# Routing by prefix-scan instructions, and table entries that serve as row numbers, in an attention, mixture-of-experts and convolution kernel

## The chip, the cores and the metric

The kernel runs on one core of one Trainium2 chip. The core has five engines that run side by side, each in its own program order: TensorE (PE, matrix products; PEld is its weight load), VectorE (DVE), ScalarE (ACT), GpSimd (POOL) and SyncE (SP, which here only issues transfers). The metric is the device time of one execution in microseconds (us); lower is better. Times are the median over separate executions; the trace and the page come from one further execution under the profiler.

## The reference, cut to what matters

Four sequences of 576 tokens pass through a windowed attention (8 heads of 64), a mixture of 8 experts with sticky routing, and a gated convolution layer. The part that the change touches is the routing:

```python
logits = x @ w_gate
for s in range(S):
    fresh_e = argmax(logits[b, s])
    if s == 0 or local_gate[b, s] < 0.5:
        e = fresh_e
    else:
        e = prev_e
    prev_e = e
    out[b, s] = p[e] * (relu(x[b, s] @ w1[e]) @ w2[e])
```

So a token keeps the expert of the last token before it that chose afresh, and each expert works on the rows of the tokens that it got.

## The kernel before, in words

Attention runs first, in a loop of 40 groups and 5 more steps, `t` = 0 to 44. Step `t` issues, in this order: the scores `s` of group t (`stage_a`, with the masked maximum `sm` on DVE, four instructions per group, two where a group is a half), the transposes `tpq`/`tpk` for the next head pair, the subtraction `sm<-sm,mx` on POOL (`stage_sub`), every fifth step the router products `lp` (`stage_l`), the transposes `pt` of group t-2 (`stage_b`), transposes `tpx` of finished rows (`stage_d`), the output products `o` of group t-3 (`stage_c`, with `rc`, a reciprocal and `xsb` on DVE where three slots are full), and the exponential of group t on ACT.

The routing of sequences 0 and 1 (`route(0)`, started at t = 25) and of 2 and 3 (`route(1)`, t = 44) is a chain of about a hundred small DVE instructions with four matrix products in it. Tokens lie as 72 partitions by 8 (`PJ`) by 2 sequences. The chain's DVE instructions wait in a list (`Later.todo`); `tick` sends one of them after certain DVE instructions of attention, and `tick(REST)` three at the end of a step. The four products are `lg` (the logits), `wp` (the running maximum carried across partitions), `bt` (counts carried across partitions) and `tb` (the table of row numbers). A product is issued when the list is empty and the loop passes the place that `PLACES` names for it: place 0 stands ahead of `pt`, place 1 ahead of `o`, place 2 behind `o`. What reads a product is issued by `early`, after two (`EVACUATE`) later calls of `passed`, of which each step has three. In the order lists this decides where each of them stands; nothing is reordered on the chip.

The running maximum over the 8 tokens of a partition is made by three shifted steps between two `scans` buffers, the running counts of the 8 experts by a copy and three shifted steps between two `ranks` buffers:

```python
for sh in (1, 2, 4):
    a, n = bufs[cur], bufs[1 - cur]
    later.tensor_tensor(out=n[:, :, 4:], in0=a[:, :, 4:], in1=a[:, :, 4 - sh : 4 + PJ - sh], op=ALU.max)
```

The table `tab` holds row number plus one, zero in an empty place. `lanes_of` and `pick1` make two index lists of it: `idx` (entry minus one, not below zero) for the gather of rows from `xD`, and `sidx` (entry minus one, and row 2304 for an empty place) for the scatter of results to `yD`, which has one row more than there are tokens.

PSUM buffers are shared by tag: `pt`, `tpx` and `bt` of `route(0)` take turns in two buffers, `s`, `lp`, `lg` and `tb` in two others, `o` and `wp` in two others.

From t = 37 on POOL gathers rows for the first expert segment (`xg`), PE turns them (`xt`), and the expert layers follow (`up`: products `h`, evacuated by ACT `hh` and DVE `hl`; `down`: products `yf` and `y`). Weights come as f32 (`wst`) and are split into two f16 halves by ACT (`wh`) and DVE (`wl`). `route(1)` runs beside the first expert segment, with PE at `h` and `yf`.

Of the kernel before, what the change touches and what calls it, by code (L numbers as in the profile page):

```python
# [10 lines left out]
F16 = mybir.dt.float16  # L11
# [11 lines left out]
N = B * S  # L23
# [41 lines left out]
PLACES = (1, 0, 0, 2)  # L65
# [22 lines left out]
def _consts():  # L88
# [38 lines left out]
    add("ie", one * np.tile(np.arange(E), 2 * PJ)[None])  # L127
    add("ik", one * np.repeat(np.arange(E), E)[None])
# [14 lines left out]
    add("tokx", np.concatenate([np.stack([(PJ * p + j) + 0.0 * b, np.full((PP, PJ), b), np.ones((PP, PJ))], -1).reshape(PP, -1) for b in range(B)], 1))  # L143
# [17 lines left out]
def attention_moe_conv_kernel(ctx: ExitStack, tc: tile.TileContext, q, k, v, w_gate, w_local, w1, w2, w_val, conv_w, w_out, consts, out):  # L161
# [4 lines left out]
    xD = dram.tile([N, D], F32, name="xD")  # L166
# [43 lines left out]
    oh_all = cp.tile([PP, B, PJ, E], F32, name="oh_all")  # L210
# [27 lines left out]
    idx8, sidx8 = r2([P, E, TILES], "idx8", I32), r2([P, E, TILES], "sidx8", I32)  # L238
# [63 lines left out]
    def cols_of(g, which):  # L302
        k, t0, n = SEGS[g]
        if k in (0, 2):
            ix = idx[k, t0 > 0][which]
            return lambda t: ix[:, t : t + 1]
        ix = (idx8, sidx8)[which]
        return lambda t: ix[:, k, t0 + t : t0 + t + 1]

    def gather(g, n=None, col=None, tiles=None):  # L310
        if col is None:
            n, col = SEGS[g][2], cols_of(g, 0)
        r = []
        for t0, m in tiles_of(n)[tiles or slice(None)]:
            x = xg.tile([P, D], F32, tag="xg", name=f"xg{g}_{t0}")
            G.indirect_dma_start(out=x[:m], out_offset=None, in_=xD[0 : 2 * S if g in (0, 1) else N, :], in_offset=bass.IndirectOffsetOnAxis(ap=col(t0 // P)[:m], axis=0))
            r.append(x)
        return r
# [41 lines left out]
    def down(g, k=None, n=None, pool=None, col=None):  # L360

        if n is None:
            k, _, n = SEGS[g]
            col = cols_of(g, 1)
# [44 lines left out]
    def turn_y(g):  # L409
        n, col = SEGS[g][2], cols_of(g, 1)  # L410
# [18 lines left out]
    if True:  # L429
# [11 lines left out]
        scans = [rt.tile([PP, 2, 4 + PJ], F32, name=f"scan{n}") for n in range(2)]  # L441
        ranks = [rt.tile([PP, 2, 4 + PJ, E], F32, name=f"ranks{n}") for n in range(2)]
# [10 lines left out]
        for u in scans:  # L453
            G.memset(u[:, :, 0:4], 0.0)
        for u in ranks:
            G.memset(u[:, :, 0:4, :], 0.0)
# [223 lines left out]
        class Later:  # L680
# [7 lines left out]
            def __getattr__(self, name):  # L688
                return getattr(Deferred(self.todo, V), name)

# [53 lines left out]
        def route(bp):  # L744
# [43 lines left out]
            later.tensor_tensor(out=dg, in0=ident[:PP, :PP].unsqueeze(1).to_broadcast([PP, 2, PP]), in1=vm[:, :, 3 + PJ : 4 + PJ].to_broadcast([PP, 2, PP]), op=ALU.mult)  # L788
# [10 lines left out]
            later.tensor_tensor(out=es, in0=vm[:, :, 4:], in1=bc(car, PJ), op=ALU.max)  # L799
            later.tensor_scalar(out=es, in0=es, scalar1=E - 1, scalar2=None, op0=ALU.bitwise_and)  # L800
            oh = oh_all[:, 2 * bp : 2 * bp + 2]
            esf = es.rearrange("p b j -> p (b j)")
            ohf = oh.rearrange("p b j e -> p (b j) e")
            ief = c("ie", PP).rearrange("p (j e) -> p j e", j=BJ)
            later.tensor_tensor(out=ohf, in0=ief, in1=bc(esf, E), op=ALU.is_equal)
# [23 lines left out]
            r3 = t([PP, 2, PJ, E], "r3")  # L829
            later.tensor_tensor(out=r3, in0=inc[:, :, 4:, :], in1=bt.unsqueeze(2).to_broadcast([PP, 2, PJ, E]), op=ALU.add)  # L830
# [5 lines left out]
            r3f = r3.rearrange("p b j e -> p (b j) e")  # L836
            later.tensor_tensor(out=r3f, in0=r3f, in1=ohf, op=ALU.mult)
            rk = rank_all[:, 2 * bp : 2 * bp + 2].rearrange("p b j -> p (b j)")
            later.tensor_reduce(out=rk, in_=r3f, axis=AX.X, op=ALU.add)
# [32 lines left out]
            for h in range(2 * bp):  # L872
# [4 lines left out]
                later.tensor_tensor(out=exps[h], in0=exps[h], in1=oh_all[:, 2 * h : 2 * h + 2].rearrange("p b j e -> p (b j) e"), op=ALU.mult)  # L877
# [6 lines left out]
        def lanes_of(nm, js, t0, t1):  # L884
# [5 lines left out]
            ixf, emp = r2([P, k, n], f"ixf{nm}"), r2([P, k, n], f"emp{nm}")  # L890
            later.tensor_reduce(out=ixf, in_=pr, axis=AX.X, op=ALU.add)
            i, o = r2([P, k, n], f"idx{nm}", I32), r2([P, k, n], f"sidx{nm}", I32)
# [737 lines left out]
```

## Time and profile before

| | |
|---|---|
| time, median of 3 executions | 459.72 us (459.29 to 461.29) |
| time of the profiled execution | 461.68 us |
| its span (first to last instruction) | 459.9 us |
| mean granted TensorE clock | 0.989 of full speed |
| busy: PE, PEld, DVE, ACT, POOL | 438.2, 326.5, 341.4, 292.6, 163.2 us |
| instructions: PE, DVE, POOL | 4618, 1006, 192 |

PE is busy for 95% of the span, so time can be won only where PE waits or where its clock is lowered. Busy time of the other engines matters where they make PE wait.

### The profile page before, as it was taken

The numbers are of one execution on the slowest core, as the hardware profiler recorded it, in microseconds if no ns is written. First come the engines' busy times: TensorE is split into PE (matmuls) and PEld (weight loads), VectorE is DVE, ScalarE is ACT, GpSimd is POOL, SyncE is SP. The second block draws the span as 40 slices with busy tenths as digits, with TensorE's granted clock in tenths as the row PEclk, the third lists the DMA queues.
The fourth block names the chain that finished last, engine by engine and source line by source line (L and its number), as shares of the span: only waits on it lengthen the run. The fifth ranks groups of instructions, "written<-read, shape, count | busy, mean of one in ns | idle before, by whom it ended". The sixth has DMA issues, their size and how long they took to land. (4 is left out here: it accounts for less than half of the span.)

```text
span 459.9 us, 12133 instructions
## 1 busy us (share of the span) xinstructions
PE 438.2 (95%) x4618; PEld 326.5 (71%) x4618; DVE 341.4 (74%) x1006; ACT 292.6 (64%) x590; POOL 163.2 (35%) x192
## 2 busy tenths in 40 slices
PE   8899999889699999999999999999999999999997
PEld 7567777556476578875788888788785857666664
DVE  5667787889758883787979898997138788779730
ACT  2887888676845233546666757767347998785532
POOL 3666665323600251402313232242005755434130
PEclk9999999899979999999999999999999999999999
DMA  9978598457637484378858897981043323020202
GB/s 212 208 173 198 130 250 201 131 143 229 216 91 261 161 273 157 96 209 274 263 181 295 277 328 232 329 275 59 9 153 103 126 71 125 24 93 1 93 21 95
DMA packets 56868, 77.79 MB, mean 169 GB/s; under 512 B 25809, under 2 KB 34017, under 8 KB 56806
## 3 DMA queue, kind: packets, MB, share of 16 engines
q1 hardware_dynamic: 53430, 67.18, 49.5%
q0 software_dynamic: 3232, 9.72, 6.1%
q8 instruction: 38, 0.62, 0.6%
q14 instruction: 24, 0.20, 0.1%
q10 hardware_dynamic: 144, 0.07, 0.1%
HBM read 62.65 MB, written 14.30 MB: 167 GB/s over the span
## 5 line engine op out<-in xcount | busy, mean ns | idle before, releaser
L347 PE MATMUL h<-xh,wh 128*128 128x256 f16 (+9 forms) x352 | 87.0, 257 | 2.5 <-DVE hl L351 2.2
L347 PE MATMUL h<-xl,wh 128*128 128x256 f16 (+9 forms) x352 | 86.9, 257 | 0.1
L347 PE MATMUL h<-xh,wl 128*128 128x256 f16 (+9 forms) x352 | 86.9, 257 | 0.0
L269 DVE SCALAR_TENSOR_TENSOR wl<-wst,wh 128x1024 f16<-128x1024 f32 x64 | 77.9, 1220 | 10.1 <-ACT wh L264 9.9
L1477 DVE SCALAR_TENSOR_TENSOR acc<-y,cw,acc 128x288 f32<-128x288 f32 x128 | 65.6, 520 | 9.2 <-ACT acc L1451 6.3
L347 PEld LDWEIGHTS <-wh 128*128 128x128 f16 x704 | 64.5, 98 | 10.9 <-issue 3.9
L264 ACT ACTIVATE wh<-wst 128x1024 f16<-128x1024 f32 x64 | 67.0, 1050 | 2.4 <-DMA wst<-in_moe_w_dram 2.4
L349 ACT ACTIVATE hh<-h 128x256 f16<-128x256 f32 (+9 forms) x88 | 30.7, 349 | 44.6 <-PE h L347 42.0
L579 POOL TENSOR_TENSOR sm<-sm,mx 128x384 f32<-128x384 f32 (+1 forms) x40 | 32.6, 815 | 52.4 <-DVE mx L571 35.2
L351 DVE SCALAR_TENSOR_TENSOR hl<-h,hh 128x256 f16<-128x256 f32 (+9 forms) x88 | 32.3, 376 | 25.4 <-ACT hh L349 24.8
L358 POOL DMA_INDIRECT yD<-yr,sidx x15 | 17.4, 1159 | 85.5 <-ACT yr L357 56.6
L396 PE MATMUL yf<-wh,hh 128*128 128x512 f16 x104 | 39.4, 379 | 0.1
L396 PE MATMUL yf<-wl,hh 128*128 128x512 f16 x104 | 39.4, 379 | 0.0
L396 PE MATMUL yf<-wh,hl 128*128 128x512 f16 x104 | 39.4, 379 | 0.0
L1507 PE MATMUL v<-yh,wv_h 128*128 128x288 f16 x128 | 36.6, 286 | 0.3 <-DVE gg L1516 0.2
L1507 PE MATMUL v<-yh,wv_l 128*128 128x288 f16 x128 | 36.6, 286 | 0.0
L1507 PE MATMUL v<-yl,wv_h 128*128 128x288 f16 x128 | 36.6, 286 | 0.0
L347 PEld LDWEIGHTS <-wl 128*128 128x128 f16 x352 | 34.6, 98 | 2.7 <-issue 0.2
L571 DVE CUSTOM_DVE_ANT_0 sm<-s,cst 128x96 f32<-128x96 f32 x144 | 29.7, 250 | 9.0 <-PE s L563 6.2
L396 PEld LDWEIGHTS <-hh 128*128 128x128 f16 x208 | 20.3, 98 | 21.1 <-issue 0.6
L380 PEld LDWEIGHTS <-wh 128*128 128x128 f16 x576 | 32.9, 97 | 2.2
L380 PE MATMUL y<-hh,wh 128*128 128x96 f16 (+6 forms) x288 | 34.3, 198 | 0.0
(260 smaller groups left out, 1059.9 us busy)
## 6 DMA issues: line engine op xcount, KB each, us to landing
wst<-in_moe_w_dram SPq DMA_DIRECT2D x64, 512.0 KB
qraw<-in_q_dram SPq DMA_DIRECT2D x16, 288.0 KB
kraw<-in_k_dram SPq DMA_DIRECT2D x16, 288.0 KB
out_dram<-ob SPq DMA_DIRECT2D x17, 256.0 KB
yg<-yD SPq DMA_DIRECT2D x16, 256.0 KB
xD<-xsb SPq DMA_DIRECT2D x2, 1152.0 KB
lraw<-in_moe_w_val_dram SPq DMA_DIRECT2D x4, 512.0 KB
lraw<-in_moe_w_out_dram SPq DMA_DIRECT2D x4, 512.0 KB
```

The costliest lines, as they stand in the source:

```text
L264: A.activation(out=wh, in_=st, func=AF.Copy, scale=SW)
L269: V.scalar_tensor_tensor(out=wl, in0=st, scalar=SW, in1=wh, op0=ALU.mult, op1=ALU.subtract)
L347: T.matmul(ps[:, :n], lhsT=w[:, fs], rhs=x[:, cc, :], start=q == 0, stop=q == 11)
L349: A.activation(out=hh[:, fc, :], in_=ps[:, :n], func=AF.Relu)
L351: V.scalar_tensor_tensor(out=hl[:, fc, :], in0=ps[:, :n], scalar=0.0, in1=hh[:, fc, :], op0=ALU.max, op1=ALU.subtract)
L358: G.indirect_dma_start(out=yD[:, :], out_offset=bass.IndirectOffsetOnAxis(ap=col(t0 // P)[:m], axis=0), in_=yr[:m], in_offset=None)
L380: T.matmul(ps[:, :r], lhsT=w[:, ds_], rhs=x[:, fc, r0:n], start=q == 0, stop=q == 23)
L396: T.matmul(ps, lhsT=x[:, fc, t0 : t0 + P], rhs=w[:, (fc % 2) * D : (fc % 2) * D + D], start=q == 0, stop=q == 23)
L571: V.tensor_tensor_reduce(out=sm[:, n, h, :], in0=ps[:, n, h, :], in1=cst[:, o + KB * mi : o + KB * mi + KB], scale=0.125, scalar=-3e38, op ...
L579: G.tensor_tensor(out=smf, in0=smf, in1=mx[:, 0 : 2 * ns].unsqueeze(2).to_broadcast([P, 2 * ns, KB]), op=ALU.subtract)
L1477: V.scalar_tensor_tensor(out=acc, in0=y32[:, cc, s0 + k : s0 + k + hw], scalar=cw[:, cc, k : k + 1], in1=acc, op0=ALU.mult, op1=ALU.add)
L1507: T.matmul(ps, lhsT=w[:, cc, cs], rhs=x[:, cc, hs], start=q == 0, stop=q == 11)
```

## The change

Each running maximum becomes one `tensor_tensor_scan` over 2 x 8 elements, each running count one over 2 x 8 x 8 elements: the instruction multiplies its state by `within` (0 at the first token of a partition's run of 8, else 1) and then takes the maximum with, or adds, the next element. For that the one-hot `oh_all` is laid out expert by expert with tokens inside, and the constant `ieb` is laid out alike; `scans` and `ranks` go. Rows of `xD` and `yD` are shifted by one: row 0 of `xD` is filled with zeros by one more transfer at t = 10, row 0 of `yD` takes what belongs to no token. The table's entry is then the row number for gather and scatter alike, and a reduction writes it as an integer at once, so that the subtractions, `emp`, `sidx` and three casts go. The constants grow by 224 columns (`ieb` and `within` 128 each, `tokx` 32 fewer). `PLACES` moves `wp` from place 0 to place 2. The loop for tokens that don't fit a segment changes alike; it is entered only where there are such tokens.

```diff
-PLACES = (1, 0, 0, 2)
+PLACES = (1, 2, 0, 2)
...
+    add("ieb", one * np.tile(np.repeat(np.arange(E), PJ), 2)[None])
+    add("within", one * (np.arange(2 * E * PJ) % PJ > 0)[None])
...
-    xD = dram.tile([N, D], F32, name="xD")
+    xD = dram.tile([N + 1, D], F32, name="xD")
...
-    oh_all = cp.tile([PP, B, PJ, E], F32, name="oh_all")
+    oh_all = cp.tile([PP, B, E, PJ], F32, name="oh_all")
...
-            row = bp * 2 * S
+            row = 1 + bp * 2 * S
...
+            def whole(self, **kw):
+                def f(**kw):
+                    with nc.allow_low_precision(reason="sums with one term that is not zero, a whole number"):
+                        V.tensor_reduce(**kw)
+
+                self.todo.append((f, kw))
...
-            bufs = scans
-            later.tensor_tensor(out=bufs[0][:, :, 4:], in0=fr.rearrange("p (b j) -> p b j", b=2), in1=fl.rearrange("p (b j) -> p b j", b=2), op=ALU.mult)
-            cur = 0
-            for sh in (1, 2, 4):
-                a, n = bufs[cur], bufs[1 - cur]
-                later.tensor_tensor(out=n[:, :, 4:], in0=a[:, :, 4:], in1=a[:, :, 4 - sh : 4 + PJ - sh], op=ALU.max)
-                cur = 1 - cur
-            vm = bufs[cur]
+            later.tensor_tensor(out=fr, in0=fr, in1=fl, op=ALU.mult)
+            vmf = t([PP, BJ], "vm")
+            later.tensor_tensor_scan(out=vmf, data0=within[:, 0:BJ], data1=fr, initial=0.0, op0=ALU.mult, op1=ALU.max)
...
-            rb = ranks
-            later.tensor_copy(out=rb[0][:, :, 4:, :], in_=oh)
-            cur = 0
-            for sh in (1, 2, 4):
-                a, n = rb[cur], rb[1 - cur]
-                later.tensor_tensor(out=n[:, :, 4:, :], in0=a[:, :, 4:, :], in1=a[:, :, 4 - sh : 4 + PJ - sh, :], op=ALU.add)
-                cur = 1 - cur
-            inc = rb[cur]
-            later.tensor_copy(out=tot_all[:, 2 * bp : 2 * bp + 2, :], in_=inc[:, :, 3 + PJ, :])
+            inc = t([PP, 2, E, PJ], "inc")
+            later.tensor_tensor_scan(out=inc.rearrange("p b e j -> p (b e j)"), data0=within, data1=oh.rearrange("p b e j -> p (b e j)"), initial=0.0, op0=ALU.mult, op1=ALU.add)
+            later.tensor_copy(out=tot_all[:, 2 * bp : 2 * bp + 2, :], in_=inc[:, :, :, PJ - 1])
...
-            later.tensor_reduce(out=ixf, in_=pr, axis=AX.X, op=ALU.add)
-            i, o = r2([P, k, n], f"idx{nm}", I32), r2([P, k, n], f"sidx{nm}", I32)
-            later.tensor_scalar(out=i, in0=ixf, scalar1=-1.0, scalar2=0.0, op0=ALU.add, op1=ALU.max)
-            later.tensor_scalar(out=emp, in0=ixf, scalar1=0.0, scalar2=float(N + 1), op0=ALU.is_equal, op1=ALU.mult)
-            later.scalar_tensor_tensor(out=o, in0=ixf, scalar=-1.0, in1=emp, op0=ALU.add, op1=ALU.add)
+            i = r2([P, k, n], f"idx{nm}", I32)
+            later.whole(out=i, in_=pr, axis=AX.X, op=ALU.add)
...
-            later.tensor_reduce(out=ek, in_=pe, axis=AX.X, op=ALU.add)
-            later.tensor_copy(out=eka[j], in_=ek)
+            later.whole(out=eka[j], in_=pe, axis=AX.X, op=ALU.add)
...
+                if t == PREP[0]:
+                    nc.sync.dma_start(out=xD[0:1, :], in_=kbd[0][0][HD : HD + 1, 0, 0, 0:D])
```

How the list of small DVE instructions empties decides in which step the products stand. On PE, at the end of step 27 and the start of step 28 (`s_1734` before and `s_1727` after are the scores of group 28), the rows of before are:

```order
L644 MATMUL tpx_1711<-cst,xsb_1475 128x128 x3
L632 MATMUL o_2_1649<-vraw3True,ph_1646 64x65 x4
L563 MATMUL s_1734<-kbd_150,qT_1289 64x192 x4
L538 MATMUL tpk_6_1745<-cst,kraw_1_1385 128x96 x3
L791 MATMUL wp_1752<-dg_1724,ones_66 72x144
L595 MATMUL pt_1754<-cst,pb_1659 96x128 x4
```

and those of the change are:

```order
L640 MATMUL tpx_1705<-cst,xsb_1467 128x128 x3
L628 MATMUL o_2_1641<-vraw3True,ph_1638 64x65 x4
L790 MATMUL wp_1718<-dg_1695,ones_66 72x144
L559 MATMUL s_1727<-kbd_145,qT_1281 64x192 x4
L534 MATMUL tpk_6_1738<-cst,kraw_1_1377 128x96 x3
L591 MATMUL pt_1745<-cst,pb_1651 96x128 x4
```

`wp` has moved ahead of the scores and of a set of transposes. The product `bt` moves in the same way from the end of the scores and transposes of step 30 to the place behind `lp` of step 29.

Also on PE, the table's product `tb` (16 products, of which the first is shown) stood behind the output products of step 34 before (`s_2039` is group 33, `s_2099` the half group 34):

```order
L632 MATMUL o_2_1949<-vraw3True,ph_1947 64x65 x4
L563 MATMUL s_2039<-kbd_146,qT_1563 64x192 x4
L538 MATMUL tpk_6_2056<-cst,kraw_1_1663 128x96 x3
L595 MATMUL pt_2063<-cst,pb_1959 96x128 x4
L644 MATMUL tpx_2070<-cst,xsb_1475 128x128 x3
L632 MATMUL o_0_2076<-vraw2False,ph_2000 64x65 x8
L563 MATMUL s_2099<-kbd_146,qT_1563 64x192 x2
L538 MATMUL tpk_7_2106<-cst,kraw_1_1663 128x96 x3
L656 MATMUL lp_2113<-xT_1876,wg 32x144 x8
L595 MATMUL pt_2123<-cst,pb_2018 96x128 x4
L632 MATMUL o_1_2138<-vraw2False,ph_2068 64x65 x4
L861 MATMUL tb_2143<-ohc_2048,ohl_2047 128x48
```

and stands behind those of step 32 now:

```order
L628 MATMUL o_2_1969<-vraw3True,ph_1967 64x65 x4
L853 LDWEIGHTS ohl_1982
L853 MATMUL tb_2032<-ohc_1983,ohl_1982 128x48
L559 MATMUL s_2051<-kbd_141,qT_1555 64x192 x4
L534 MATMUL tpk_6_2062<-cst,kraw_1_1655 128x96 x3
```

All PE work of steps 33 and 34 now stands behind `tb`. On DVE, what `tb` reads (`ohl`, `ohc`) is made between the score evacuations (`sm`) of step 32; before, it was made in step 33. These are the rows of the change:

```order
L705 SCALAR_TENSOR_TENSOR ln_1900<-td_1899,rank_all 72x16
L705 SCALAR_TENSOR_TENSOR cl_1901<-es_1759,td_1899 72x16
L705 TENSOR_TENSOR ohc_1983<-cols,cl_1901 72x768
L705 TENSOR_TENSOR ohl_1982<-lanes,ln_1900 72x512
L567 ISA sm_1991,mx_1992<-s_1986,cst 128x96
L567 ISA mx_1992 128x1
L705 TENSOR_TENSOR ohl_1982<-lanes,ln_1900 72x512
...
L705 TENSOR_TENSOR ohc_1983<-ohc_1983,sv_74 72x768
L529 COPY qT_1861<-tpq_4_2001 128x96x3
```

The last row that `tb` needs is the second `ohc`, behind the fourth `sm` of step 32.

## Rows read from the trace of the kernel before

**Rows 1.** Busy time by stage: window, length, PE, PEld, DVE, ACT, POOL, clock, DMA share, GB/s.
```profile
34.50:46.00 11.50, 11.50 (x168) 8.84 (x165) 8.92 (x50) 8.63 (x17) 7.47 (x10) 1.00 0.87 198
...
80.50:92.00 11.50, 9.58 (x114) 6.65 (x111) 9.65 (x59) 7.34 (x17) 4.13 (x6) 0.85 0.45 131
...
126.50:138.00 11.50, 11.04 (x94) 8.29 (x95) 6.84 (x12) 4.65 (x9) 0.00 (x0) 0.71 0.31 91
...
190.00:230.00 40.00, 40.00 (x369) 28.61 (x367) 32.95 (x57) 24.16 (x42) 8.71 (x8) 1.00 0.72 221
```

**Rows 2.** Timeline of PE, steps 28 and 29: start, length, [idle before <- releaser].
```profile
83.81 0.47 PE L791 MATMUL wp<-dg,ones 72*72 72x144 f32 x2 [1.52 <-DVE dg L702]
...
85.58 0.86 PE L563 MATMUL s<-kbd,qT 128*64 128x192 f32 x4
```

**Rows 3.** Timeline of DVE and POOL ahead of that product.
```profile
81.81 1.40 DVE L702 TENSOR_TENSOR scan<-scan 72x16 f32<-72x16 f32 x2
...
81.57 0.83 POOL L579 TENSOR_TENSOR sm<-sm,mx 128x384 f32<-128x384 f32 x1 [1.37 <-DVE scan L702]
82.36 0.82 POOL L483 TENSOR_TENSOR qside<-qraw,one 96x384 f32<-96x384 f32 x1
```

**Rows 4.** Routing's instructions on DVE: count, least/median/longest ns, first and last start.
```profile
L702 DVE TENSOR_TENSOR scan<-scan x6: 161/171/749, 81.8 to 142.9; 72x16 f32<-72x16 f32 x6
L702 DVE TENSOR_TENSOR ranks<-ranks x6: 277/284/289, 87.1 to 148.5; 72x128 f32<-72x128 f32 x6
```

**Rows 5.** Timeline of PE and DVE, step 30.
```profile
92.47 0.55 PE L644 MATMUL tpx<-cst,xsb 128*128 128x128 f32 x3 [0.86 <-DVE ph L600]
...
94.58 0.27 DVE L702 TENSOR_TENSOR r<-ranks,bt 72x128 f32<-72x128 f32 x1
```

**Rows 6.** Timeline of DVE and POOL, step 32.
```profile
96.68 0.82 DVE L702 TENSOR_TENSOR pe<-sel,cst 128x8 f32<-128x8 f32 x1
...
96.64 0.83 POOL L579 TENSOR_TENSOR sm<-sm,mx 128x384 f32<-128x384 f32 x1 [2.82 <-DVE sel L702]
```

**Rows 7.** Timeline of PE, steps 33 and 34.
```profile
98.04 0.82 PE L563 MATMUL s<-kbd,qT 128*64 128x192 f32 x8
...
101.06 0.52 PE L644 MATMUL tpx<-cst,xsb 128*128 128x128 f32 x3 [1.12 <-DVE cmpt L702]
...
103.92 0.72 PE L656 MATMUL lp<-xT,wg 128*32 128x144 f32 x16 [0.99 <-DVE mx L571]
...
105.95 1.72 PE L861 MATMUL tb<-ohc,ohl 72*128 72x48 f16 x16
```

**Rows 8.** Timeline of DVE: first score evacuation of steps 31, 35, 36, 37 and 39.
```profile
95.49 0.25 DVE L571 CUSTOM_DVE_ANT_0 sm<-s,cst 128x96 f32<-128x96 f32 x1
...
109.51 0.25 DVE L571 CUSTOM_DVE_ANT_0 sm<-s,cst 128x96 f32<-128x96 f32 x1
...
112.34 0.26 DVE L571 CUSTOM_DVE_ANT_0 sm<-s,cst 128x96 f32<-128x96 f32 x1
...
115.55 0.26 DVE L571 CUSTOM_DVE_ANT_0 sm<-s,cst 128x96 f32<-128x96 f32 x1
...
119.22 0.26 DVE L571 CUSTOM_DVE_ANT_0 sm<-s,cst 128x96 f32<-128x96 f32 x1
```

**Rows 9.** The page's group of weight splits on DVE: busy, mean ns, idle before.
```profile
L269 DVE SCALAR_TENSOR_TENSOR wl<-wst,wh 128x1024 f16<-128x1024 f32 x64 | 77.9, 1220 | 10.1 <-ACT wh L264 9.9
```

**Rows 10.** Timeline of PE: the transposes of the third gather's rows.
```profile
126.96 1.09 PE L328 MATMUL xt<-cst,xg 128*128 128x128 f32 x4 [2.10 <-DMA xg<-xD,idxa]
```

**Rows 11.** Timeline of PE beside the second routing.
```profile
149.08 0.17 PE L821 MATMUL bt<-tot_all,triu 72*72 72x8 f16 x1 [0.62 <-DVE tot_all L702]
...
154.28 1.74 PE L861 MATMUL tb<-ohc,ohl 72*128 72x48 f16 x16 [0.59 <-DVE ohc L702]
...
168.42 0.25 PE L347 MATMUL h<-xh,wh 128*128 128x208 f16 x1 [1.02 <-DVE hl L351]
```

**Rows 12.** PE's clock in one microsecond of step 29: length, PE busy, clock, DMA share, GB/s.
```profile
86.00:87.00 1.00, 1.00 (x7) 0.50 0.79 243
```

More of the change, by code (lines that the diff above doesn't have):

```diff
@@ L142, in _consts @@
     add("xtri", one * (np.arange(E)[:, None] > np.arange(E)[None, :]).astype(np.float32).reshape(1, -1))
-    add("tokx", np.concatenate([np.stack([(PJ * p + j) + 0.0 * b, np.full((PP, PJ), b), np.ones((PP, PJ))], -1).reshape(PP, -1) for b in range(B)], 1))
+    add("tokx", np.concatenate([np.stack([(PJ * p + j) + 1.0, np.full((PP, PJ), b)], -1).reshape(PP, -1) for b in range(B)], 1))
     return np.concatenate(cols, 1), off
@@ L300, in tiles_of, with cols_of @@
         return [(t0, min(P, n - t0)) for t0 in range(0, n, P)]
-    def cols_of(g, which):
+    def cols_of(g):
         k, t0, n = SEGS[g]
         if k in (0, 2):
-            ix = idx[k, t0 > 0][which]
+            ix = idx[k, t0 > 0]
             return lambda t: ix[:, t : t + 1]
-        ix = (idx8, sidx8)[which]
-        return lambda t: ix[:, k, t0 + t : t0 + t + 1]
+        return lambda t: idx8[:, k, t0 + t : t0 + t + 1]
     def gather(g, n=None, col=None, tiles=None):
         if col is None:
-            n, col = SEGS[g][2], cols_of(g, 0)
+            n, col = SEGS[g][2], cols_of(g)
         r = []
@@ L315, in gather @@
             x = xg.tile([P, D], F32, tag="xg", name=f"xg{g}_{t0}")
-            G.indirect_dma_start(out=x[:m], out_offset=None, in_=xD[0 : 2 * S if g in (0, 1) else N, :], in_offset=bass.IndirectOffsetOnAxis(ap=col(t0 // P)[:m], axis=0))
+            G.indirect_dma_start(out=x[:m], out_offset=None, in_=xD[0 : 2 * S + 1 if g in (0, 1) else N + 1, :], in_offset=bass.IndirectOffsetOnAxis(ap=col(t0 // P)[:m], axis=0))
             r.append(x)
@@ L363, in down @@
             k, _, n = SEGS[g]
[L364 removed]
+            col = cols_of(g)
         hh, hl = hts.pop(g)
@@ L440, in attention_moe_conv_kernel @@
         raw, sides, vsp, qk, stiles, ptiles, pts, otile, xsb, xT, lacc = {}, {}, {}, {}, {}, {}, {}, {}, {}, {}, {}
-        scans = [rt.tile([PP, 2, 4 + PJ], F32, name=f"scan{n}") for n in range(2)]
-        ranks = [rt.tile([PP, 2, 4 + PJ, E], F32, name=f"ranks{n}") for n in range(2)]
+        within = c("within", PP)
         kbd = []
@@ L828, in route @@
             yield "s"
-            r3 = t([PP, 2, PJ, E], "r3")
-            later.tensor_tensor(out=r3, in0=inc[:, :, 4:, :], in1=bt.unsqueeze(2).to_broadcast([PP, 2, PJ, E]), op=ALU.add)
+            r3 = t([PP, 2, E, PJ], "r3")
+            later.tensor_tensor(out=r3, in0=inc, in1=bt.unsqueeze(3).to_broadcast([PP, 2, E, PJ]), op=ALU.add)
             if bp == 0:
@@ L835, in route @@
             yield "now"
-            r3f = r3.rearrange("p b j e -> p (b j) e")
-            later.tensor_tensor(out=r3f, in0=r3f, in1=ohf, op=ALU.mult)
+            later.tensor_tensor(out=r3, in0=r3, in1=oh, op=ALU.mult)
             rk = rank_all[:, 2 * bp : 2 * bp + 2].rearrange("p b j -> p (b j)")
-            later.tensor_reduce(out=rk, in_=r3f, axis=AX.X, op=ALU.add)
+            later.tensor_reduce(out=rank_all[:, 2 * bp : 2 * bp + 2], in_=r3.rearrange("p b e j -> p b j e"), axis=AX.X, op=ALU.add)
             yield "e"
@@ L876, in route @@
                 later.reciprocal(out=se, in_=se)
-                later.tensor_tensor(out=exps[h], in0=exps[h], in1=oh_all[:, 2 * h : 2 * h + 2].rearrange("p b j e -> p (b j) e"), op=ALU.mult)
+                eh = exps[h].rearrange("p (b j) e -> p b j e", b=2)
+                later.tensor_tensor(out=eh, in0=eh, in1=oh_all[:, 2 * h : 2 * h + 2].rearrange("p b e j -> p b j e"), op=ALU.mult)
                 pe = p_all[:, 2 * h : 2 * h + 2].rearrange("p b j -> p (b j)")
@@ L956, in pick1 @@
             pe8 = r2([P, E, E], "pe8")
-            ekf = r2([P, E], "ekf")
             later.tensor_tensor(out=pe8, in0=sel, in1=c("ie")[:, 0:E].unsqueeze(1).to_broadcast([P, E, E]), op=ALU.mult)
-            later.tensor_reduce(out=ekf, in_=pe8, axis=AX.X, op=ALU.add)
-            later.tensor_copy(out=eki, in_=ekf)
+            later.whole(out=eki, in_=pe8, axis=AX.X, op=ALU.add)
             yield "e"
@@ L965, in pick1 @@
                 later.tensor_tensor(out=pr4, in0=sel[:, k0:k1, :].unsqueeze(2).to_broadcast([P, n, TILES, E]), in1=tabv[:, 0:TILES, :].unsqueeze(1).to_broadcast([P, n, TILES, E]), op=ALU.mult)
[L966 to L971 removed]
+                later.whole(out=idx8[:, k0:k1, :], in_=pr4, axis=AX.X, op=ALU.add)
             yield "e"
@@ L1323, in attention_moe_conv_kernel @@
         V.memset(slot, 0.0)
-        tokc = rx([PP, BJ4, 3], "tokc", F16)
-        V.tensor_copy(out=tokc, in_=c("tokx", PP).rearrange("p (n three) -> p n three", three=3))
+        tokc = rx([PP, BJ4, 2], "tokc", F16)
+        V.tensor_copy(out=tokc, in_=c("tokx", PP).rearrange("p (n two) -> p n two", two=2))
         lo1s = [rx([PP, P], f"lo1_{n}", F16) for n in range(4)]
@@ L1374, in attention_moe_conv_kernel @@
                 drain(up("x", E, P, xc))
-                drain(down("x", E, P, xc, lambda t: xs_))
+                drain(down("x", E, P, xc, lambda t: xx))
                 V.tensor_scalar(out=slot, in0=slot, scalar1=1.0, scalar2=None, op0=ALU.add)
@@ L1397, in fetch @@
         g = gp.tile([P, D], F32, tag="yg", name=f"yg{b}{t}", bufs=6)
-        nc.sync.dma_start(out=g[:m], in_=yD[b * S + t * P : b * S + t * P + m, :])
+        nc.sync.dma_start(out=g[:m], in_=yD[1 + b * S + t * P : 1 + b * S + t * P + m, :])
         fetched.append(g)
```

38 lines of the change are left out of this document (12 added, 26 removed).

## The prediction, made before the changed kernel ran

> **What bounds the kernel now.** I read first the busy time by stage, to see where PE has anything to lose. From 190 us on it is busy in every microsecond, and in 34.5 to 46 us too; in 80.5 to 92 us it is busy for 9.58 of 11.5 us, with a mean clock of 0.85, while DVE is busy for 9.65 [rows 1]. So the time is decided by PE everywhere but in the stretch in which the first routing runs beside attention, and by that stretch alone can this change win or lose much: nothing that it touches is PE work of size. Next I read PE's timeline there, row by row with what released it, and beside it those of DVE and POOL. The reader is to see that PE's waits have routing behind them (1.52 us for `wp`, 0.86 in step 30, 1.12 and 0.99 in steps 33 and 34) [rows 2, 5, 7], and that DVE stands still in places where its own work would take a fifth of the time, because POOL is reading SBUF just then.
>
> **What goes.** A shifted step over 16 elements takes 171 ns, one over 128 elements 284 ns [rows 4]. Per routing go two small steps net (three, less the new scan), and of four operations on 128 elements (the copy and three steps) three. The index lists lose three instructions of the small kind in the first routing, nine in the second, and three casts go. Small ones that follow one another start 0.1 to 0.2 us apart, so DVE gets about 1.2 us of work less in the first routing and 2.0 in the second. PE gets nothing less.
>
> **What a scan costs.** No row shows one. From below it is the row of a step of its size (0.17 and 0.28 us), from above twice that (0.34 and 0.57), since each element waits for the one before it. I take 0.2 and 0.4, between them; both ends are 0.1 us apart per scan and don't move the sum. [...]
>
> **What hides the rest.** 224 more columns of constants are 115 KB, about 0.6 us at the 198 GB/s of their stretch; PE is busy there throughout [rows 1], so they cost nothing, and 0.6 us if that cover were gone. The 2 KB for row 0 of `xD` is one more issue on SP, 20 steps before anything reads it. Shifted rows are as long as before. In the late part gathers and scatters read the same number of rows.
>
> **Step 27 to 28: `wp`.** After its copy of `qT`, DVE's two shifted steps took 1.40 us for 0.34 us of work, since POOL's subtraction (81.57 to 82.40) and then `qside` (82.36 to 83.18) stood in the way of one each [rows 3]. In the change the scan stands where the first of them stood and `dg` where the second did: both read two operands from SBUF, so `dg` ends at about 83.4, and `wp` starts at 83.45 in place of 83.81 [rows 2, 3]. But the scores and transposes of step 28, which PE did ahead of its wait (1.2 us, up to 82.29) [rows 2], now stand behind `wp`. PE idles from 81.2, for 2.25 us in place of 1.52, and reaches `pt` of step 28 later by 1.2 less 0.36, some 0.9 us; the scores of step 29 start at 86.45, not 85.58 [rows 2]. The lower clock that follows (0.50) [rows 12] stays, as the wait ahead of it grew.
>
> **Steps 29 to 31.** `bt` now stands in step 29, where no `tpx` needs the second `pt` buffer, so the 0.86 us of step 30 go [rows 5], and PE is level again at step 31. DVE isn't: `r` to `key` (0.9 us, from 94.58 on) [rows 5] now come ahead of the scores of step 30, and eleven small instructions follow beside them, among them `pe`, which took 0.82 us for 0.16 beside a subtraction on POOL [rows 6]. I get 96.5 us for the first score evacuation of step 31, against 95.49 [rows 8]; but by then DVE has done routing work that it did in steps 32 and 33 before.
>
> **Step 32: `tb`, the term that decides.** From 96.5 on DVE has ahead of `tb`: eight score evacuations (1.45 us), five small instructions (0.6), one block by POOL's subtraction (0.7, by the excess of `pe`) [rows 6], two `ohc` and four `ohl` (2.3). That is 5.1 us, so `tb` can start at 101.7. PE has done step 32 at 98.2, as it had before, when the scores of step 33 started at 98.04 with no wait since `tpx` of step 30 [rows 5, 7]. So it waits 3.5 us, then does `tb` (1.72) and has 103.4 where it had 98.04 before the work of steps 33 and 34. That work took 7.9 us, up to the old `tb` at 105.95, of which 2.1 were waits [rows 7]; those go, so it ends at 109.2. DVE can take the last outputs from about 109.0 on (0.9 us), splits two weights (1.2 us each) [rows 9], has 0.4 us of routing left and comes to the scores of step 35 at 112.6, against 109.51 [rows 8].
>
> **Steps 35 to 39.** Here the gain is paid out. Between 109.51 and 112.34 DVE took 2.83 us for score evacuations, one output evacuation and the table's read and lists; between 112.34 and 115.55 3.21 us, of which the four evacuations and one split explain 1.9 [rows 8, 9]. Most of the rest has been done by now or is gone: 1.2 us and 1.3 us less, and another 0.2. DVE needs 7.0 us in place of 9.71 to step 39 [rows 8] and is there at 119.6, 0.4 later than before; call it 0.2, as some of PE's and ACT's waits there go too. POOL's gathers follow the subtractions, so they move with it, and PE's 2.10 us at 126.96 for the third gather [rows 10] end 0.2 us later too.
>
> **The clock.** Two waits of PE in this stretch were followed by a granted clock of 0.50: the 1.52 us of step 28 and the 2.10 us at the gather [rows 2, 10, 12], and the second lowered the mean of the stage from 126.5 us on to 0.71 [rows 1]. The new wait of 3.5 us is longer than both. At the low clock the half group's scores take 0.86 us [rows 2], and some 3.4 us at that clock hold about 1.9 us of such work: 1.5 us lost, on PE just where DVE waits for PE. I count it once.
>
> **The second routing.** PE waits 0.62, 0.59 and 1.02 us [rows 11]. `bt` stands six products earlier, 1.3 us, and `tot_all` is ready some 2 us earlier (0.5 us less work in the counts, and no split of weights, 1.2 us [rows 9], with an `hl` of 0.3 in between): 0.62 us gained. `tb` keeps some 0.45 of its 0.59. The third wait came from routing between two `hl`; now a block of routing stands ahead of the first `hl` of that segment (some 30 instructions, 0.1 to 0.5 us apart, that ran in part behind it before), and by their sum PE waits some 0.95 us at the fourth `h` in place of 1.02 at a later one. Gain 0.85 us in all.
>
> **Sum.** Profiled execution 461.68 us: +0.2 (first routing), +1.5 (clock), -0.85 (second routing) = 462.5. That execution was 2.0 us above the median of the three timed ones, 459.72, so the forecast is 460.5 on their scale: no change that can be told, where 0.5% (2.3 us) is about what a measurement can tell.
>
> **Rivals.**
> *Faster: DVE's saving goes through.* If POOL doesn't block the scan, `dg`, `pe` and `cl`, DVE is 1.5 to 2 us earlier at `tb`, PE's wait is 1.5 us and no low clock follows it. Then steps 35 to 39 keep the 2.7 us of lighter DVE work, less the 0.4 by which they would start late, and the second routing adds 0.85: 459.7 - 3 = 456.7. For it: DVE is the busiest engine here. [...] Chance 0.22.
> *Slower: the low clock lasts.* If it stays down after `tb` as it did after the gather, through steps 33 to 35, PE loses 1.5 us once more and reaches the gather late, and the gather's own low clock comes on top: 460.5 + 1.5 to 2.5 = 462 to 463. [...] For it: the stage from 126.5 us, with a mean of 0.71 over 11.5 us [rows 1], spent some 6.7 us at half clock. Chance 0.28.
> *No low clock after `tb`:* 459.7 - 0.65 = 459.1; inside the forecast.
> *Hidden anyway:* the stretch is set by the gather and by weights in flight, and both kernels meet at 126.96: 459.7 less 0.85 at most; inside the forecast too.
>
> **Chances and range.** No change by over 0.5%: 0.50 (forecast, no low clock, hidden), faster 0.22, slower 0.28. The range leaves out the outer halves of both rivals: 457.0 to 463.0. The likeliest case alone holds 458.5 to 462.
>
> **What would show it.** Right: PE waits for `dg` at `wp` about 2.2 us, for `ohc` at the first `tb` 2.5 to 3.5 us, with the clock lowered within a few us; no wait at `tpx` of step 30; scores of step 35 on DVE later than 109.5, those of step 39 within 1 us of 119.2; no wait at the second `bt`, one of about 1 us at the fourth `h` of that segment. Wrong: a scan over 128 elements above 0.6 us; `tb` of the first routing with a wait under 1 us; a new wait for constants or `qraw` before 46 us; PE's products after 190 us no longer back to back.

## The result, and the profile after

The changed kernel takes 463.54 us (median of 20 executions, 458.86 to 466.45); the kernel before, beside it, 459.35 us (457.04 to 464.43). The ratio is 1.0066, with a 95% interval of 1.0042 to 1.0091: slower by two thirds of a per cent, past the 0.5% that can be told apart, and 0.5 us above the end of the predicted range. The mean times, 463.10 and 459.83 us, are 3.3 us apart, the medians 4.2. The profiled execution has a span of 461.4 us (459.9 before) and the same mean granted clock as the one of before, 0.989.

The stages of the changed kernel, to be read against [rows 1]. Columns: window, length, PE, PEld, DVE, ACT, POOL, clock, DMA share, GB/s.

```profile
34.50:46.00 11.50, 11.09 (x154) 8.21 (x147) 8.49 (x45) 7.96 (x16) 6.64 (x10) 1.00 0.74 185
80.50:92.00 11.50, 9.09 (x124) 6.69 (x121) 9.65 (x50) 8.11 (x17) 4.78 (x7) 1.00 0.58 161
92.00:103.50 11.50, 7.55 (x101) 6.32 (x100) 11.04 (x59) 6.90 (x15) 3.76 (x6) 0.89 0.63 182
103.50:115.00 11.50, 10.47 (x121) 7.37 (x119) 7.21 (x36) 8.82 (x15) 1.33 (x2) 0.82 0.27 81
...
126.50:138.00 11.50, 9.50 (x114) 7.20 (x111) 8.60 (x16) 7.07 (x15) 0.92 (x2) 1.00 0.51 136
...
149.50:161.00 11.50, 8.92 (x43) 4.38 (x42) 10.19 (x34) 2.53 (x4) 1.01 (x1) 0.85 0.47 161
...
190.00:230.00 40.00, 39.95 (x375) 28.93 (x373) 32.48 (x56) 24.11 (x43) 8.16 (x8) 1.00 0.69 214
```

From 190 us on PE is as busy as before. The low clock has moved: it was in the windows from 80.5 and from 126.5 us of [rows 1] (0.85 and 0.71), and both are now at 1.00; it is low from 92 to 115 us, and from 149.5 to 161.

PE's timeline at the two routings, with the row of the third gather and the product `lg` of the second routing between them:

```profile
84.75 0.47 PE L790 MATMUL wp<-dg,ones 72*72 72x144 f32 x2 [2.17 <-DVE dg L705]
...
92.40 0.49 PE L640 MATMUL tpx<-cst,xsb 128*128 128x128 f32 x3
...
102.11 1.69 PE L853 MATMUL tb<-ohc,ohl 72*128 72x48 f16 x16 [3.57 <-DVE ohc L705]
103.73 1.55 PE L559 MATMUL s<-kbd,qT 128*64 128x192 f32 x8
...
129.60 0.63 PE L329 MATMUL xt<-cst,xg 128*128 128x128 f32 x4 [1.31 <-DMA xg<-xD,idxa]
...
139.13 0.65 PE L753 MATMUL lg<-cst,lacc 128*72 128x36 f32 x8
...
147.01 0.17 PE L814 MATMUL bt<-tot_all,triu 72*72 72x8 f16 x1
...
154.20 1.75 PE L853 MATMUL tb<-ohc,ohl 72*128 72x48 f16 x16 [2.58 <-DVE ohc L705]
```

What was 1.52, 0.86, 1.12 and 0.99 us in four places [rows 2, 5, 7] is 2.17 and 3.57 us in two. The clock fell while PE still stood in the second of these waits: it reads 0.96 from 100 to 101 us and 0.50 from 101 to 102. The scores behind the first `tb` then took 1.55 us where they took 0.82 [rows 7]. In the second routing `bt` waits for nothing (0.62 before [rows 11]); `tb` waits 2.58 us (0.59 before), and starts at the same time as before, with six products of `yf` that stood ahead of it now behind it.

DVE's timeline in the changed kernel: the scan and `dg` of each routing (with POOL's two instructions beside the first pair), the long scan, and the first scores of steps 33, 35 and 39, to be read against [rows 3, 4, 8].

```profile
83.16 0.64 DVE L705 TENSOR_TENSOR_SCAN vm<-cst,fr 72x16 f32<-72x16 f32 x1
83.83 0.86 DVE L705 TENSOR_TENSOR dg<-cst,vm 72x144 f32<-72x144 f32 x1
...
82.92 0.83 POOL L575 TENSOR_TENSOR sm<-sm,mx 128x384 f32<-128x384 f32 x1 [1.37 <-DVE fr L705]
83.70 0.82 POOL L479 TENSOR_TENSOR qside<-qraw,one 96x384 f32<-96x384 f32 x1
...
88.70 0.42 DVE L705 TENSOR_TENSOR_SCAN inc<-cst,oh_all 72x128 f32<-72x128 f32 x1
...
105.79 0.26 DVE L567 CUSTOM_DVE_ANT_0 sm<-s,cst 128x96 f32<-128x96 f32 x1 [2.48 <-PE s L559]
...
114.36 0.24 DVE L567 CUSTOM_DVE_ANT_0 sm<-s,cst 128x96 f32<-128x96 f32 x1
...
122.80 0.24 DVE L567 CUSTOM_DVE_ANT_0 sm<-s,cst 128x96 f32<-128x96 f32 x1
...
142.49 0.18 DVE L705 TENSOR_TENSOR_SCAN vm<-cst,fr 72x16 f32<-72x16 f32 x1
142.70 0.31 DVE L705 TENSOR_TENSOR dg<-cst,vm 72x144 f32<-72x144 f32 x1
```

The scan costs 0.18 us over 16 elements and 0.42 over 128. Beside POOL the first took 0.64 and `dg` 0.86 (0.31 in the second routing). DVE comes to step 39 at 122.80, 3.58 us later than before [rows 8]; of this 1.35 us were there at step 27 already. Yet both kernels are level at 139.1 us, since the changed one has no low clock behind the gather (1.00 from 126.5 to 138 us, 0.71 before). The same product in the trace of before:

```profile
139.12 0.65 PE L750 MATMUL lg<-cst,lacc 128*72 128x36 f32 x8
```

In this pair of executions the 1.5 us come behind that point, where the second routing is.

One pair of executions doesn't show the loss, though: it is one of many that differ in clock. Every execution has its own span and mean granted clock, and these tell more. Below, "lost" is (1 - mean clock) x span, the time that the clock took from PE if it never waited, with the standard error of its mean. These means are over every execution, while the ratios leave out those more than 1.5% above the fastest of their kernel, mostly ones that lost much to the clock (three of 20 of the change, two of 12 of `old_order`, three of the six of `shift_only`, below), so that where the two differ the means tell more.

```
kernel                 executions   mean span   lost, us    clock 0.992 or more
before (three groups)      76         458.7     3.0 +-0.2        60
the change                 20         461.3     7.6 +-0.6         1
```

The kernel before lost 2.4 to 3.4 us in each of its three groups; for its executions beside the change no clock was kept. Inside a kernel, an execution that lost 1 us more was 0.86 us longer (common slope of all kernels here, with a standard error of 0.04; a correlation: it does not tell which of the two brings the other). By it 4.7 us more lost account for 4.0 us, which is more than the mean times differ by (3.3 us) and as much as the medians do (4.2). **By this the change's loss is time at the low clock**; an estimate from the same figures is that at equal clock the change would be about 1 us faster than the kernel before. The question is what lowers the clock.

### The profile page after: what moved, and what is told of

The parts are those of the page before. It is cut to its first block, busy times and chain, and to the rows that moved or that the text cites. A ratio compares the mean times of both kernels' runs of the same rounds, so it can differ in the third digit from the quotient of the medians.

```text
span 461.4 us, 12104 instructions
## 1 busy us (share of the span) xinstructions
PE 436.6 (95%) x4618; PEld 324.9 (70%) x4618; DVE 338.8 (73%) x981; ACT 292.1 (63%) x590; POOL 162.5 (35%) x188
## 5 line engine op out<-in xcount | busy, mean ns | idle before, releaser
L359 POOL DMA_INDIRECT yD<-yr,idx x15 | 18.2, 1216 | 84.4 <-ACT yr L358 56.3
```

## The experiments

Each was timed in alternation with the kernel before; ratios are to that. A hold that several use, on the changed kernel: the product number n waits at least until step HOLD[n], called a slot from 45 on, behind the attention loop (1 to 3 are `wp`, `bt`, `tb` of the first routing, 5 and 6 `bt` and `tb` of the second).

```diff
+HOLD = {6: 53}
...
-                if self.at == "m" and not self.todo and (place is None or place == PLACES[self.made]):
+                if self.at == "m" and not self.todo and self.step >= HOLD.get(self.made, 0) and (place is None or place == PLACES[self.made]):
...
+                later.step = t
```

**The two `tb` alone.** The theory after the result was that the two `tb` placed before their operands carry the loss, and of these the second. HOLD was {6: 53}, {3: 34} and both.

> The change, with only the second routing's `tb` held back by one loop slot, to slot 53, where it stood before. Theory (the two early `tb` carry the loss, and only the second one's lasts): PE no longer waits 2.58 us in slot 52, the wait of 1.02 us at an `h` may come back, and the kernel is 1 to 2.5 us faster than the change, 0.1 to 0.5% above the kernel before. Rival A (the larger constants and row 0 make the first 46 us late by 1.35 us): no faster than the change. Rival B (the scans and their blocks by POOL cost it): no faster than the change either.

> The change, with only the first routing's `tb` held back to step 34, place 2, where it stood before. Theory (the first wait is paid back at the gather, the second lasts): PE's wait of 3.57 us in step 32 goes to under 1 us, but PE waits about 2 us at the third gather again and the clock falls there again; the time is that of the change within 0.7 us. If instead the first wait is not paid back: 2 to 3.5 us faster than the change. Rivals A and B: within 0.3 us of the change.

> The change, with both `tb` held back to where they stood before (step 34, slot 53). Theory: 1 to 2.5 us faster than the change, as with the second alone, 0.0 to 0.4% above the kernel before; what stays is up to 0.6 us at the start for the constants. If both waits last: 3.5 to 5 us faster than the change, and 0.5 to 2 us faster than the kernel before. Rivals A and B: as slow as the change.

Measured: 1.0050 (1.0013 to 1.0087), 1.0123 (1.0068 to 1.0179) and 1.0073 (1.0035 to 1.0110). The theory fell: neither the one nor both give the loss back. Only the first, with the second `tb` held, comes near what was expected of it (0.5% above the kernel before, and 5.9 us lost for the change's 7.6), and the one with the first `tb` held came out slower than the change. Rivals A and B forecast no gain, and these three runs leave them standing. PE's timeline with both held shows why the holds don't help:

```profile
83.92 0.47 PE L791 MATMUL wp<-dg,ones 72*72 72x144 f32 x2 [2.16 <-DVE dg L706]
...
102.64 0.67 PE L641 MATMUL tpx<-cst,xsb 128*128 128x128 f32 x3 [2.29 <-DVE xsb L610]
...
151.69 1.73 PE L854 MATMUL tb<-ohc,ohl 72*128 72x48 f16 x16 [1.66 <-DVE ohc L706]
```

The wait doesn't go, it moves to the next instruction that DVE has to serve. `wp` and `bt` come a step earlier, so DVE has `ohc` and `ohl` ahead of the `qT` and `xsb` that PE wants next (from 97.5 to 101.2 us), and PE stands still for that, whichever product comes next. In the second routing PE, no longer held at `bt`, reaches `tb` ahead of DVE in slot 53 as well.

**The constants.** Without the 256 added columns; both `tb` early as in the change.

```diff
-    add("ieb", one * np.tile(np.repeat(np.arange(E), PJ), 2)[None])
-    add("within", one * (np.arange(2 * E * PJ) % PJ > 0)[None])
...
-        within = c("within", PP)
+        within = rt.tile([PP, 2 * E * PJ], F32, name="within")
+        G.memset(within, 1.0)
+        G.memset(within.rearrange("p (n j) -> p n j", j=PJ)[:, :, 0:1], 0.0)
...
-            ief = c("ieb", PP).rearrange("p (b e j) -> p b e j", b=2, e=E)
+            ief = c("ie", PP)[:, 0:E].unsqueeze(1).unsqueeze(3).to_broadcast([PP, 2, E, PJ])
```

> The change without the 256 added columns of constants: the one-hot comparison reads the eight numbers of `ie` broadcast, and `within` is made by two memsets on POOL. Both `tb` stay early. Rival A (constants make the start late): the waits of PE and DVE between 40 and 46 us go back to those of the kernel before, and the kernel is 0.6 to 1.4 us faster than the change. Theory: 0 to 0.5 us faster, since PE is busy there; the waits of 3.57 and 2.58 us at the two `tb` stay.

Measured: 1.0127 (1.0074 to 1.0180), no gain; that it came out slower than the change, on six executions, stays unexplained. PE's wait of 0.40 us at 45.79 us in the change's trace is gone here (PE is busy for 11.50 of the 11.50 us from 34.5 on), and that changes nothing: PE reached `wp` at 81.59 us here and at 81.55 with the added columns in the kernel with `tb` held to slot 53, against 82.58 in the change. The 1.35 us are a difference between executions, not the constants. Rival A falls.

**Order against content.** Theory 2: the loss comes from the order of PE's products, which turns several short waits into few long ones. `shift_only` has the rows' shift and the shorter lists on the kernel before, and no scan; its products stand as before. `old_order` has all of the change, with every product where it stood before:

```diff
-PLACES = (1, 2, 0, 2)
+PLACES = (1, 0, 0, 2)
...
+HOLD = {1: 28, 2: 30, 3: 34, 5: 50, 6: 53}
```

> The kernel before with the shift alone: rows of x and y one later, the row of zeros, table entries as row numbers, the shorter lists; running maximum and counts stay shifted steps, and all routing products stay where they stood before. Theory 2 (the loss is more time at the low granted clock, called by longer single waits of PE that come with the scans' order of products): mean granted clock as before (0.990 to 0.996), time 0 to 1 us below the kernel before. Rival (row 0, unaligned rows or the gathers cost it): as slow as the change, 0.5% or more above the kernel before, at an unchanged clock.

> The change with all of its instructions, but every routing product of PE held where it stood before: `wp` in step 28 place 0, `bt` in step 30, `tb` in step 34, and slots 50 and 53. Theory 2: the waits are spread again (about 1.5, 0.9, 1 us), mean granted clock 0.990 to 0.996, time within 0.3% of the kernel before or up to 1.5 us below it. Rival (DVE's instructions bunch whatever the products' places): a wait of over 2 us stays between 97 and 107 us, mean clock 0.983 to 0.988, 0.5 to 1% above the kernel before, as with the two `tb` alone held back.

`old_order` measured 458.96 us beside 460.61: 0.9936 (0.9898 to 0.9974), **faster than both kernels**, and 0.64% faster than the one before. Over all of its 12 executions the mean span is 1.7 +-1.0 us below the kernel before, so the gain on that kernel is less sure than the gain on the change. It lost 2.6 us to the clock. Rival B falls by it: the scans are there, and `dg` is blocked as in the change (0.87 us). Its stages:

```profile
80.50:92.00 11.50, 9.53 (x125) 7.07 (x125) 10.67 (x56) 8.34 (x17) 5.60 (x8) 1.00 0.49 136
92.00:103.50 11.50, 9.52 (x137) 6.96 (x135) 10.27 (x59) 9.02 (x18) 2.89 (x6) 1.00 0.56 155
103.50:115.00 11.50, 9.88 (x135) 7.23 (x124) 10.11 (x45) 8.39 (x15) 3.56 (x4) 1.00 0.71 231
...
149.50:161.00 11.50, 10.68 (x79) 7.19 (x78) 10.23 (x35) 4.61 (x7) 4.86 (x3) 1.00 0.35 126
```

And its PE at the places where the change waits 2.17, 3.57 and 2.58 us:

```profile
84.38 0.47 PE L791 MATMUL wp<-dg,ones 72*72 72x144 f32 x2 [1.11 <-DVE dg L706]
...
91.75 0.55 PE L641 MATMUL tpx<-cst,xsb 128*128 128x128 f32 x3 [0.78 <-DVE ph L597]
...
100.33 0.52 PE L641 MATMUL tpx<-cst,xsb 128*128 128x128 f32 x3 [1.11 <-DVE td L706]
103.06 0.72 PE L653 MATMUL lp<-xT,wg 128*32 128x144 f32 x16 [0.88 <-DVE mx L568]
...
152.47 1.73 PE L854 MATMUL tb<-ohc,ohl 72*128 72x48 f16 x16 [0.82 <-DVE ohc L706]
```

PE is busy for 9.52 us from 92 to 103.5, against 7.55 in the change, at a clock of 1.00, against 0.89. `shift_only` gave 0.9898 (0.9820 to 0.9976), on few executions; over all six its mean span is 0.7 us below the kernel before beside it, and it lost 3.0 us. So no cost of the shift shows, with an error of 1.5 us; how much of the gain is its own stays open.

**Later still.** `late55` holds only the second `tb`, to slot 55; `smooth` puts every product where its operand should be ready (`wp` step 28 place 1, `bt` step 30, `tb` step 35, slots 50 and 55).

> The change with the second routing's `tb` held back to slot 55, three slots later than the change has it, so that DVE's `ohc` is done first. Theory 2: no wait at that `tb`, no low clock from 154 to 159 us, which each of the five kernels with a wait of 1.5 to 2.8 us there shows; mean granted clock 0.003 to 0.007 above the change's 0.983, and 1.2 to 2.8 us faster than the change, 0 to 0.4% above the kernel before. If that wait is not what lowers the clock: clock and time as the change.

> The change with every product where its operand should be ready: `wp` in step 28 at place 1, `bt` in step 30, `tb` in step 35, slots 50 and 55. Theory 2: no wait of PE over 1.5 us for routing, mean granted clock 0.993 or above, 0.5 to 2.5 us below the kernel before. Rival (waits only move to the next instruction that needs DVE): PE waits 2 us or more for scores or outputs in steps 32 to 34, clock below 0.99, no faster than the kernel before.

`late55` measured 1.0049 (1.0012 to 1.0085). Its clock is 1.00 from 149.5 to 161 us, as expected, and the lost time falls to 5.8 us. But the gain is not the 1.2 to 2.8 us expected, since PE waits behind it for the same DVE:

```profile
149.50:161.00 11.50, 11.50 (x85) 7.78 (x84) 8.82 (x26) 4.61 (x7) 4.80 (x3) 1.00 0.51 171
...
164.81 0.25 PE L349 MATMUL h<-xh,wh 128*128 128x208 f16 x1 [1.44 <-DVE hl L353]
...
168.42 0.25 PE L349 MATMUL h<-xh,wh 128*128 128x208 f16 x1 [1.08 <-DVE hl L353]
```

`smooth` measured 1.0113 (1.0053 to 1.0172), and lost 6.8 us. Its rival was right about the time and the clock, but not about the 2 us: no wait of PE for DVE in the first routing is above 1.46 us. So theory 2 had its condition, no long wait for routing, and missed the clock all the same: shorter waits can go with a low clock too. The kernel has the same two waits at `h` (1.42 and 1.09 us), and PE waits three times for ACT just behind the first routing, with low clock from 111 to 119 us:

```profile
107.96 0.64 PE L592 MATMUL pt<-cst,pb 128*96 128x128 f32 x4 [1.30 <-ACT pb L583]
109.43 0.55 PE L641 MATMUL tpx<-cst,xsb 128*128 128x128 f32 x3 [0.83 <-ACT ph L595]
111.45 0.45 PE L629 MATMUL o<-vraw3False,ph 96*64 96x65 f32 x8 [1.09 <-ACT vraw3False L505]
```

A product held too long only handed its wait on.

**Which routing.** `old_first` holds the first routing's three products as before ({1: 28, 2: 30, 3: 34}, old PLACES), `old_second` the second's two ({5: 50, 6: 53}), `wp_late` only `wp` ({1: 28}, old PLACES), and `old_few` is `old_order` without the added constants.

> The change with the first routing's products held where they stood before (`wp` step 28 place 0, `bt` step 30, `tb` step 34), the second routing's as the change has them (slots 49 and 52). Theory 2, with the loss split: the two single waits of 2.2 and 3.6 us go and with them their low clock; a wait of 1.5 to 2.6 us at `tb` in slot 52 and low clock after it stay. Mean granted clock 0.989 to 0.992, time 1.5 to 3.5 us below the change, within 0.4% of the kernel before. If the second routing carried the loss alone: as slow as the change.

> The change with the second routing's products held where they stood before (slots 50 and 53), the first routing's as the change has them. Theory 2: the waits of 2.2 us at `wp` and 3.6 us at `tb` and the low clock after them stay, the wait at the second `tb` falls below 1 us. Mean granted clock 0.985 to 0.989, time 1 to 2 us below the change, 0.2 to 0.6% above the kernel before. If the second routing carried the loss alone: 0.2 to 0.7% below the kernel before.

> The change with only `wp` held back to where it stood before (step 28, place 0); the products behind it follow as soon as they may (`bt` step 29, `tb` step 32, slots 49 and 52). The wait at `wp` falls from 2.2 to about 1.1 us. If it is the wait at `tb` in step 32 that costs most (theory 2 as it stands): that wait stays at 3 us or more, low clock follows it, and time and clock are those of the change within 1 us. If it is the wait at `wp`: 2 us or more faster than the change.

> All of the change's products where they stood before, and no added columns of constants (the comparison reads `ie` broadcast, `within` by two memsets on POOL). If the constants cost nothing, as predicted: the time of the same kernel with the constants (0.36 to 1.0% below the kernel before) within 0.5 us. If they cost at the start what the first 46 us of the change's trace show (1.35 us late): 0.5 to 1.4 us faster still.

Ratios: 1.0069 (1.0031 to 1.0108), 1.0038 (0.9998 to 1.0078), 1.0088 (1.0050 to 1.0125) and 0.9962 (0.9930 to 0.9994). Over every execution, with the mean span against that of the kernel before beside it:

```
first routing   second routing   kernel        lost, us     span against before
as before       as before        old_order     2.6 +-1.0        -1.7
as before       as before        old_few       2.7 +-0.7        -0.7
as before       early            old_first     5.0 +-1.0        +2.7
early           as before        old_second    5.3 +-0.5        +3.2
early           early            the change    7.6 +-0.6        +3.3 (mean times)
```

In the profiled execution of `old_second` the first routing's stages have the clock of the change, and PE waits there as in the change; in that of `old_first` they have that of `old_order`. Their stages from 92 us on, `old_second` first:

```profile
92.00:103.50 11.50, 7.56 (x98) 6.27 (x99) 10.22 (x54) 6.21 (x13) 3.76 (x6) 0.86 0.70 209
103.50:115.00 11.50, 10.62 (x134) 7.57 (x133) 7.84 (x40) 8.83 (x15) 1.67 (x3) 0.84 0.24 77
```

```profile
92.00:103.50 11.50, 9.52 (x135) 6.92 (x136) 10.58 (x59) 9.18 (x19) 2.88 (x6) 1.00 0.61 156
103.50:115.00 11.50, 9.94 (x125) 7.48 (x126) 11.12 (x53) 9.06 (x16) 3.65 (x5) 1.00 0.72 230
```

Either routing's early products lose some 2.5 us to the clock, and both some 5.0: in lost time the two parts add up. In span they don't: above `old_order` either alone costs 4.4 and 4.9 us, and both 5.0, each with an error of over 1 us. So `old_first` missed the 1.5 to 3.5 us that it was expected to gain on the change (1.0069 against 1.0066), and holding one routing alone back gains nothing in mean span. By the slope of 0.86 that leaves 1 to 2 us that either half costs besides the clock, and no run here says where. `wp_late` shows that holding `wp` alone gives no time back: its wait falls to 1.11 us, `tb` keeps 3.57, and the ratio is no better than the change's. Its lost time, 5.5 +-0.5 us, is below the change's, so that `wp` has no part in the clock's loss is not shown. `old_few` agrees with `old_order` within their intervals: the constants cost nothing that shows here.

**Waits and low clock, profile by profile.** One profiled execution of each kernel (of `late_tb0` the longest of its six); waits in us, and where the granted clock of a microsecond was below 1.00.

```
kernel       at wp   longest, 97-107   second tb   low clock
before       1.52    1.12              0.59        85-89, 126-134
shift_only   1.51    0.99              0.59        124-129, 455-457
old_order    1.11    1.11              0.82        125-132
old_few      1.11    1.11              1.82        152-156
old_first    1.09    1.11              2.27        124-132
the change   2.17    3.57              2.58        100-108, 155-159
late_tb1     2.17    3.57              1.52        99-107, 154-158
few_consts   2.16    3.57              2.00        83-88, 100-108, 155-159
late55       2.16    3.57              none        85-89, 102-110
old_second   2.16    3.57              0.82        100-108, 155-159
wp_late      1.11    3.57              2.92        100-108, 155-159
late_both    2.16    2.29              1.66        102-107, 154-158
late_tb0     2.16    2.29              2.84        84-92, 105-112, 156-164
smooth       none    1.11              none        111-119, 129-136
```

Each of the eight kernels with a wait of 2.29 us or more between 97 and 107 us had its clock lowered there; of the other six only `smooth` did, later. At the second `tb` the clock fell in seven of eight with 1.5 us or more, and in one of six with less. At `wp` it fell after 2.16 us in three kernels of seven. So a long wait doesn't lower the clock each time; in these profiles the fall is commoner behind one. At the gather it fell in four of the five kernels with the first routing in its old order and in `smooth`, and in none of the eight with it early: in the change the transposes there wait 0.69, 0.69 and 1.31 us, where they waited 2.10 in one [rows 10].

## Why the prediction was right and wrong

- **What a scan costs**: 0.2 and 0.4 us predicted, 0.18 and 0.42 measured. Against a shifted step (0.17 and 0.28 [rows 4]) the 112 further elements take 2.1 ns each in place of 1.0, twice a step's, as the prediction's upper end had it for the whole instruction.
- **What hides the rest**: right. The constants cost nothing that could be told, with either order.
- **Step 27 to 28**: right; 2.25 us predicted at `wp`, 2.17 measured. That the low clock behind it stays was wrong in this execution, and in four of seven.
- **Steps 29 to 32**: right; no wait at `tpx` of step 30, and 3.57 us at `tb` for 3.5 predicted, for the reason given (DVE's work in one piece).
- **Steps 35 to 39**: predicted 112.6 and 119.6 us for the scores of steps 35 and 39, measured 114.36 and 122.80. That is 1.8 and 3.2 us late; the start's 1.35 us and the 1.5 us of clock, which the text counted apart, make 2.85, so the sum of DVE's work was right within 1.1 us.
- **The second routing** is the first step that failed. "Gain 0.85 us in all" took `tb` to stay in slot 53; it goes to slot 52, ahead of six more products of `yf`. The wait predicted for the fourth `h` came there, with low clock behind it. With the first routing early in both, holding the second one's products back takes the lost time from 7.6 to 5.3 us; with the first as before, from 5.0 to 2.6. The term was a loss of some 2 us by the slope of 0.86, where a gain of 0.85 had been put; in mean span it can't be told from nothing with the first routing early, and is 4.4 us with the first as before.
- **The clock** is the second. "I count it once", 1.5 us, and as if the falls of before stayed. The stretch at the low clock that it takes is the one behind `wp` in the trace of before: 0.68, 0.50, 0.50 and 0.61 in the four microseconds from 85 us on, which at half clock make 3.4 us. At the first `tb` of the change it is 0.96, six times 0.50 and 0.62 from 100 us on, which make 6.8. The sum was made on a profiled execution of before with clock falls in two places and a mean of 0.989, while 60 of 76 executions of that kernel were at 0.992 or above: the falls differ from execution to execution, and the change raises what they cost in the mean, from 3.0 to 7.6 us lost. The rival "the low clock lasts" (462 to 463 us, chance 0.28) named the clock as what costs the time, and is the nearest to 463.54, but looked for it behind the first `tb` alone. Its other half was wrong: the gather's low clock did not come on top, and in all eight profiles with the first routing early there is none there.
- **The faster rival** had 456.7 us, 3.0 below before. `old_order`, which keeps every wait of routing at 1.11 us or less, is 2.9 us below by its ratio (1.2 to 4.7) and 1.7 by its mean span; `old_few` is 1.7 and 0.7 below. So the change's arithmetic is worth some 1 to 3 us where the order lets it through. That the rival's time is near is luck: its condition, that POOL blocks nothing, does not hold in `old_order`, where `dg` is blocked as well (0.87 us). What stood against the gain was the order.

What stays open: why one execution with a wait of 2.27 us at the second `tb` kept its clock; why `smooth` lost 6.8 us without a long wait for routing; and why either early routing alone costs as much span as both, though it loses half as much to the clock.

## What to carry to other kernels

Making one engine's work shorter in a program whose order follows from readiness also moves the other engine's products: look at where the waits go, not only at the work saved, and undo the moves by themselves before the edit is given up. Four waits of 0.8 to 1.1 us in the first routing of `old_order` were cheaper here than the two of 2.2 and 3.6 us in the change: the waits themselves differ by 1.9 us (3.9 against 5.7), and the early order lost some 2.6 us more to the clock besides. Short waits alone were no safeguard: `smooth` lost 6.8 us with no wait of PE for DVE above 1.46 us in either routing. And before a per cent is explained from one trace, compare the mean granted clock of all the executions: the profiled executions of these two kernels agree in clock (0.989), and the kernels differ in the mean (3.0 and 7.6 us lost).

## What the runs showed of the hardware

A single execution loses from nothing to some 12 us to the clock with the same program (mean clock 1.000 to 0.974 in the 12 executions of `old_order`), and spans of one kernel follow it at 0.86 us per us lost. No run shows what makes the difference between executions of one program. No profile here shows a low clock before 83 us (the earliest is 0.90 from 83 to 84 us, in `few_consts`); here it is the falls in the middle of the kernel that go with a difference of 0.7% (3.0 and 7.6 us lost).

The sum over a strided view took longer: `rank_all`, taken from the expert-major layout, 0.39 us against 0.28 before for the same 128 elements (0.38 against 0.28 in the second routing). The first row is that of before:

```profile
95.21 0.28 DVE L702 TENSOR_REDUCE rank_all<-r 72x16 f32<-72x128 f32 x1
...
92.17 0.39 DVE L705 TENSOR_REDUCE rank_all<-r 72x16 f32<-72x128 f32 x1
```
